# One plan replaced by another: new order, engines and buffer slots for the same instructions of an attention and SwiGLU kernel

## The chip, the core and the metric

The kernel runs on one NeuronCore of a Trainium2 chip. The metric is the device time of one execution in microseconds (us). The core has five engines, each of which works through a queue of its own in order: PE (TensorE, matrix products into PSUM), DVE (VectorE), ACT (ScalarE), POOL (GpSimd) and SP (SyncE, which here only issues DMAs). Engines wait for each other through semaphores. PSUM has eight banks of 128 x 512 float32.

## The reference

Four sequences of 768 positions and eight heads of 64 go through causal attention; heads 0, 2 and 6 see all earlier keys, the others only the first four keys and a window of 64. Its output, 3072 tokens of 512 values, goes through a SwiGLU block of width 1536.

```python
scores = scale * np.matmul(q, k.transpose(0, 1, 3, 2))
...
stream_keep = causal & (is_sink | in_win)
mask = np.where(retr[0, :, 0, 0, None, None], full_mask, stream_mask)
scores = np.where(mask[None, :, :, :], scores, -1000000000.0)
scores = scores - np.max(scores, axis=-1, keepdims=True)
a = np.exp(scores)
a = a / (np.sum(a, axis=-1, keepdims=True) + 1e-09)
return np.matmul(a, v).astype(np.float32)
...
g = x @ w_gate
silu = g * (1.0 / (1.0 + np.exp(-g)))
val = x @ w_val
return (silu * val @ w_out).astype(np.float32)
```

## The kernel before

The work is written as 1071 tasks. `P.add` (in class `Plan`) makes a task with a name, the engines that may do it, what it depends on and the ring of buffers it takes; no task runs at that point. At the end `P.order()` reads three strings: `ORDER` (two characters for each number of a task, in the sequence of emission; numbers from 3700 on are extra warming matmuls), `WAYS` (one digit for each task: which of its engines) and `SLOTS` (one digit for each buffer taken). The loop in the last lines of the kernel emits the tasks in that order. Every engine's queue is therefore the subsequence of `ORDER` that falls to it, and the three strings alone set what waits behind what. Semaphore waits follow from the tiles that tasks share.

Tokens come in 24 tiles of 128 (tile t), two to a pair n (twelve pairs), four to a group g (six groups). A tile's or pair's batch and place follow from `QP`; for instance tiles 8 to 11 are the last four tiles of batch 1 and make group 2, and tiles 12 to 17 belong to batch 2. The tasks' names, as the text uses them:

- `load q5`, `load k5`, `load x5` (x is v), `load g0`, `load v0`, `load o0` (the three weights): DMAs of 512 KB each, issued by SP into a ring of eleven raw buffers (L349 to L362).
- `cq5`, `ck5`, `cx5.0.0`, `wc g0`: casts of raw float32 to float16 (L206 on ACT, L208 on POOL or DVE, L212 as a reduction on DVE).
- `trq`, `trk` and `evq`, `evk`: for pairs 0 to 4, turning of q and k by PE (L473) and evacuation by ACT or DVE. For pairs 5 to 11, `dq5.0`, `dk5.0` are transposing DMAs instead (L463), issued by SP.
- `sc8.0`: scores of a tile, units of up to eight blocks (PE, L567); `ex8.0`: exponentials (ACT, L579); `mask8.0`: product with a 0/1 mask (DVE or POOL, L587); `sk1.2`, `sv1.2`: copies of the sink keys and values into a later tile's place; `val8.1`, `val8.0`: products with v (PE, L597); `nm8`: division by the row sum (DVE, L604 and L605), into a ring of three xb buffers.
- `xtr0` and `xe0`: for tiles 0 to 7, turning of the result by PE (L621) and evacuation. For tiles 8 to 23, `xdma8` is a transposing DMA from SP (L615) into xt.
- `gate2.11`, `vals2.11`: the two products of the SwiGLU block for group 2, column block 11 (PE, L759, four matmuls); `tanh` (ACT, L765), `stt1`, `stt2` (DVE, L769 and L775) make h from them. All gates of a group need the xt of all its four tiles.
- `out1.p1` to `out1.p7`: the output product of a group in seven products by Strassen's scheme (PE, L845, twelve matmuls of 128 x 256 each). `hs1.1` to `hs1.4`, in two parts each (L826, DVE or POOL), are the sums of h that it needs, `ws` (L412) those of w_out; `oe1.r1`, `oe1.c11` and so on gather the products into out_sb (L866 and L859 on DVE, or L206 on ACT); `st1.h0`, `st1.h1` store the halves of a group's result (L883, from SP's or ACT's DMA queue), `st5.*` the pieces of the last group (L874).

PSUM's banks are shared out by `SLOTS`: scores and values take two banks ("big"), a gate, a product or a turning one. Who takes a bank waits until its last user is done with it.

```python
    for number in P.order():
        if number < P.FILL:
            running.append(P.tasks[number])
            P.tasks[number].run()
        else:
            warm((number - P.FILL) % 16, (number - P.FILL) // 16)
```

Of the kernel before, what the change touches and what calls it, by code (L numbers as in the profile page):

```python
# [13 lines left out]


ORDER = (
    "0602070300090A0804010D1U1V1cy11W1X0C1d1f0B2021y01g0g281e1i22231h2B1j290m1r2A0h1Y2C1p1Z1b0F2D1q1a"
    "2L2X0n1s1k1l2N1m2W2M2f051t0G2g1u2O1w2E1v242c2F252h1n1y262d1z272e2i2G2H1o2j0E0z2l2I2P2Q0y2m8o2R2t"
    "2J0k8e118p2K2U8q8f102x2o2V302y8g0i138r8h8s0q318j8i8m2n8k8y323C0H932k8t8l148z3I2p9098943J2S1x9D3D"
    "95918n8u8w929E9G0o388v3K9F3L0j992Z8x963M9H2Y339A0l3R97343U3N1C9B2b2q9C2r0I3S2z9h2u2s3V9c0J2a169i"  # L20
    "3O3W9d9j353P3b369e9N1D373X0r3E3f3l3F393n3m9k0p3Q3g9f3T9O9l3h3Y3Z0s3o9I3a173i9g0K2v1F3j3A190u9L9J"
    "0v3u3d9r2w3c0x3G3k9S0w9K3v9P9Q3H9T9M0M9m9s1G9U3e409t9n431A9R413p9u3B440L9o453q9v429X3r0P4C49464D"
    "3s9Y9V4A9Z189p3t479W4H9a9q2T3x4N4Q4K4B4RBE4V9b4O0tAu1HAzAv48BF0OBH9y3y9zAV4LAw0NB21QB0BG4ZAx4M1R"
    "0R1EAQAy1TB1ApAW4g5D1B4YAY1512AkBI5KAXB4Aq1K4eArB7B51SAZAl0Q9w5CAm0W3zB30SAn3w1M4f4bB9Ao1OAR4h4E"
    "AS4FA44P4I4G5IB69xAa1N5fA54i4lB84j5mAsA01IBAAdAt0Y4mA20V4S4T1J5H5LALA1AbA3AT5G4U5JA74cA8BB5lAcAM"
    "4dBCAU4a1P4JA95gAfBD1LAA5oAg4vAe4kAh5n4q56ANAC57AB0X4r4W5E5F0T514y4o52ADAE4p4nA64sAF4t4zAHAG4w4u"
    "AK545TAI5W5553AOAJ505X4xAiAP5c4X5U58Aj59BL5sBJ5A5tBN5B6wBM5M5p5vBP5NBR0U5YBO0eBKBQ0bBX5q5V6v5r5Z"
    "BV6ICb5hBW6PBU5k5aBZ5bCc6H5OBSBsCd6NCMBt6J5uBuBi745wBYBvBjBaBT6OCNBbBw60CO72CeBcBk71CCCfBlCDBd0a"
    "7PCH0ZBm6QCE666369CI67CJCF7364CK68CG6E5P5QCWCL6A5i5dC75j65815R5x5yCZ5zCX5S61C86UCY6R0fCP6SC96y5e"
    "CaC27OCQ6B62C36e6T6CBn6VC47W6DCABo6F6zBpBx6GCB707F6Z6W0cC56aBhBy7UBq7GC6BzCR6K0dBr6n756X6xCiBe6Y"  # L30
    "6o6M6b6c76CU6fCSD57R77CTD86dDtCVBf7H7879DuC0D6DeBgCk6gC1D7DA7X7A80DjDvDm89CjDkD9DfDl7CDhDnDB857D"
    "DUDgDiDPDV7L6LDWDwDCDQ7b6h83DX6i7ECg7cDYDxDR6k6p7Y6lCm87DS6jCh7I7J7V6qDD7K7M7ZDy7BDE6mDT6rDzDZ86"
    "Cl6sDaE17j6t7dCo7Q6uE0CnDK7NE2DoCpDL88Db7aCsDMDp7sCtDr7tDq7e7m7p7fDN7q7g7nDO7h7rDcEhDdCq7iCuEi7k"
    "Ds7xDFEj82CvCr8I8D8ADGDIDH8B8NCw8J7l7oEwCxDJCyEx7S7T8EEXCz8FEy8G8TEYD0EkE5EZD47u7v8HEz7wE67yD1El"
    "8U8CFLF0D2E3FMFNE88KE48LFB8M8O8V8Q8Y8P8W8RFG847zESE7FH8XFOFCEAEf8ZFPFDFEETF9FFD38SEcEU8aEaEdEe8b"
    "F6Eg8cEuF7FI8dEmE9EBELEEECEbErF1EsEtEFEvF2EVEGEDEpEWEHF8FAEnF4EoFJEqF3EJEIFKFpEKFTGTENGHGUFqGiFr"
    "FsGVF5GbFtEOFVEMGEEPG4GWG5GFG6GYEQFSG7GGGZFUG2GIGaGJGcGOGKG8GMGLGPERGXFzGjGQGRGkGNFQFxFXFRFWG0FY"
    "GSG1FcFaFuFbG9FvFwFiFyG3FeFZFdGdFfFlGeGpGAFjGrGlGBFmGCGfFnGgGDGmFgGhGnFhFkGvGqFoGsGtH1GxGuGzGyGo"
    "GwH3H0HCH2H5H4HAHDH7H8H6HEH9HBHFHG"
)  # L40
WAYS = (
    "000000000000000000000000000000000000000000000000000000000000222222202021222202210011111100110001"
    "212201000100000000000000120002212221011000000000000000001100222210000011000000000001101000000000"
    "001000020202010001000000000000010010010010000000002001020000000000010000012000000100000000000002"
    "000000100000000000200000000000000001020000000010000000000000200000200000000100100000210001001000"
    "000200000020000001001000000001000000100000000001222000000100000000010000102010210000001001000002"
    "200010010000012020212200000010010000000120000001000000000000000000000000000000000000000000000000"
    "000000000000000000000000000000000000000000000000000100000000000000000000000000000000000000000000"
    "000000000000000000000000000000000000000110000000000010000000000000000000000000000000000000000000"
    "000000000000000000001111010011000000000001100000000000000000000000000000000000000000000000000000"  # L50
    "000000000111101000000000000000110000000000000000000000000000000000000000000000000000000000000001"
    "100000110000000000010000000000000000000000000000000000000000000000000000000000000000010000001000"
    "000000000001101"
)
# [1001 lines left out]
```

## Time and profile before

| | us |
|---|---|
| median of 3 runs | 242.46 (241.78 to 242.67) |
| the profiled execution | 242.79 |
| its span, first to last instruction | 241.0 |
| PE busy | 232.1 |
| DVE, ACT, POOL busy | 185.0, 146.0, 127.6 |
| granted TensorE clock, mean | 0.997 |

Times in the trace count from the start of the span. A row of the order of time gives start, length, engine, line, operation, out<-in, form and count, and in brackets how long the engine was idle before it and what ended that. Consecutive like instructions are merged into one row. Issues of DMAs stand under SPq or ACTq: their length is the time in which the queue is held by the issue, not that of the transfer. A row of the waits reads: who waited for whom, us in total, times, longest.

### The profile page before, as it was taken

The numbers are of one execution on the slowest core, as the hardware profiler recorded it, in microseconds if no ns is written. First come the engines' busy times: TensorE is split into PE (matmuls) and PEld (weight loads), VectorE is DVE, ScalarE is ACT, GpSimd is POOL, SyncE is SP. The second block draws the span as 40 slices with busy tenths as digits, with TensorE's granted clock in tenths as the row PEclk, the third lists the DMA queues.
The fourth block names the chain that finished last, engine by engine and source line by source line (L and its number), as shares of the span: only waits on it lengthen the run. The fifth ranks groups of instructions, "written<-read, shape, count | busy, mean of one in ns | idle before, by whom it ended". The sixth has DMA issues, their size and how long they took to land.

```text
span 241.0 us, 5649 instructions
## 1 busy us (share of the span) xinstructions
PE 232.1 (96%) x2211; PEld 146.3 (61%) x2211; DVE 185.0 (77%) x344; ACT 146.0 (61%) x223; POOL 127.6 (53%) x144
## 2 busy tenths in 40 slices
PE   7999999999999998799999999999999999999993
PEld 2677865654566867455564466666746665467783
DVE  2679998989899985498946987568646897875984
ACT  3599999879888878659774684655761111421100
POOL 7395878563957402926969519598960020214220
PEclk9999999999999999999999999999999999999998
DMA  6999999999999979989887414202031000220224
GB/s 184 354 340 366 335 334 366 356 334 305 205 257 167 191 182 252 269 145 213 172 162 223 94 22 89 44 5 77 35 104 51 0 0 0 90 88 0 90 101 162
DMA packets 67179, 40.74 MB, mean 169 GB/s; under 512 B 25168, under 2 KB 61008, under 8 KB 67152
## 3 DMA queue, kind: packets, MB, share of 16 engines
q1 hardware_dynamic: 64832, 36.58, 60.9%
q10 hardware_dynamic: 2320, 3.80, 4.3%
q8 instruction: 17, 0.28, 0.5%
q14 instruction: 10, 0.08, 0.1%
HBM read 28.31 MB, written 6.29 MB: 144 GB/s over the span
## 4 chain that ended last, share of the span: by engine, by line
PE 85%; DVE 5%; DMA 3%; SPq 2%; ACT 1%; issue 1%; POOL 0%; DVEq 0%; POOLq 0%; ACTq 0%
PE banks L759 51%; PE banks L845 17%; PE banks L567 7%; PE banks L597 5%; DMA xt<-xb 3%; PE banks L321 3%; PE banks L473 2%; SPq L615 2%; ACT e L579 1%; DVE out_sb L866 1%; DVE h_sb L775 1%; DVE sil L769 1%; PE banks L621 1%; DVE xb L605 1%; DVE h_sb L826 0%
## 5 line engine op out<-in xcount | busy, mean ns | idle before, releaser
L765 ACT ACTIVATE sig<-banks 128x512 f32<-128x512 f32 (+1 forms) x76 | 42.4, 575 | 53.5 <-PE banks L759 45.9
L759 PE MATMUL banks<-xt,wg_sb 128*128 128x512 f16 (+1 forms) x304 | 71.0, 368 | 1.5 <-DMA xt<-xb 1.5
L759 PE MATMUL banks<-xt,wv_sb 128*128 128x512 f16 (+1 forms) x304 | 71.5, 368 | 0.0
L579 ACT ACTIVATE e<-banks 128x1024 f16<-128x1024 f32 (+2 forms) x68 | 60.0, 912 | 13.4 <-PE banks L567 8.9
L769 DVE SCALAR_TENSOR_TENSOR sil<-sig,banks 128x512 f32<-128x512 f32 (+1 forms) x76 | 48.8, 654 | 15.1 <-ACT sig L765 14.6
L775 DVE SCALAR_TENSOR_TENSOR h_sb<-sil,banks 128x512 f16<-128x512 f32 (+1 forms) x76 | 48.9, 655 | 11.0 <-PE banks L759 9.6
L587 POOL TENSOR_TENSOR e<-e,m 128x640 f16<-128x640 f16 (+1 forms) x22 | 38.0, 1729 | 26.7 <-ACT e L579 24.4
L845 PEld LDWEIGHTS <-h_sb 128*128 128x128 f16 x432 | 41.6, 98 | 9.4 <-DVE h_sb L826 0.2
L759 PEld LDWEIGHTS <-wg_sb 128*128 128x128 f16 x304 | 28.7, 98 | 28.5 <-DMA xt<-xb 1.8
L759 PEld LDWEIGHTS <-wv_sb 128*128 128x128 f16 x304 | 27.9, 98 | 26.8
L826 POOL TENSOR_TENSOR h_sb<-h_sb 128x768 f16<-128x768 f16 x14 | 22.9, 1640 | 31.2 <-DVE hs_sb L826 12.6
L866 DVE TENSOR_TENSOR out_sb<-banks,out_sb 128x512 f32<-128x512 f32 x41 | 27.8, 687 | 7.5 <-PE banks L845 5.8
L845 PE MATMUL banks<-wo_sb,h_sb 128*128 128x256 f16 x216 | 26.4, 273 | 0.0
L845 PE MATMUL banks<-wt_sb,h_sb 128*128 128x256 f16 x216 | 26.3, 273 | 0.0
L567 PE MATMUL banks<-qT,kT 64*128 64x128 f16 x472 | 20.3, 218 | 1.2 <-ACT qT L206 0.6
L567 PEld LDWEIGHTS <-kT 64*128 64x128 f16 x472 | 14.5, 94 | 11.0 <-issue 10.4
L597 PEld LDWEIGHTS <-e 128*128 128x128 f16 x472 | 17.5, 97 | 5.8 <-issue 1.3
L597 PE MATMUL banks<-vt,e 128*128 128x65 f16 x472 | 18.9, 193 | 0.9 <-ACT e L579 0.9
L206 ACT CAST hq<-raw 128x1024 f16<-128x1024 f32 (+1 forms) x17 | 15.9, 945 | 5.2 <-DMA raw<-in_q_dram 4.4
L826 POOL TENSOR_TENSOR hs_sb<-h_sb 128x768 f16<-128x768 f16 x5 | 8.2, 1639 | 20.0 <-DVE h_sb L775 20.0
L605 DVE TENSOR_TENSOR xb<-banks,rc 128x512 f16<-128x512 f32 x24 | 16.6, 691 | 1.8 <-DMA xt<-xb 1.0
L208 POOL CAST vt<-raw 64x512 f16<-64x512 f32 x22 | 13.4, 608 | 2.4 <-DMA raw<-in_v_dram 1.1
(58 smaller groups left out, 185.3 us busy)
## 6 DMA issues: line engine op xcount, KB each, us to landing
raw<-in_v_dram SPq DMA_DIRECT2D x12, 512.0 KB, 6.0
raw<-in_q_dram SPq DMA_DIRECT2D x8, 512.0 KB, 5.2
raw<-in_k_dram SPq DMA_DIRECT2D x8, 512.0 KB, 6.3
raw<-in_moe_w_gate_dram SPq DMA_DIRECT2D x6, 512.0 KB, 8.3
raw<-in_moe_w_val_dram SPq DMA_DIRECT2D x6, 512.0 KB, 8.5
raw<-in_moe_w_out_dram SPq DMA_DIRECT2D x6, 512.0 KB, 8.5
out_dram<-out_sb ACTq DMA_DIRECT2D x6, 512.0 KB, 2.8
raw<-in_q_dram SPq DMA_DIRECT2D x8, 256.0 KB, 6.4
```

The source lines that it names most:

```text
L567: nc.tensor.matmul(sc[:, c:c + n, :], weights, moving, start=first, stop=last)
L579: nc.scalar.activation(out=to, in_=src, func=AF.Exp, scale=scale)
L587: ENG[task().way].tensor_tensor(out=ev, in0=ev, in1=mm, op=ALU.mult)
L597: nc.tensor.matmul(avs[t][:, odd, n * 66:n * 66 + 65], ee, vv, start=(m == 0), stop=(m == len(bl) - 1))
L605: nc.vector.tensor_tensor(out=xb.rearrange("p n o d -> p o n d"), in0=av[:, :, :, 0:64], in1=rc.to_broadcast([128, 2, 4, 64]), op=ALU.mult)
L759: nc.tensor.matmul(ps, wsb[:, kk, j * 128:(j + 1) * 128], xt[:, kk, c[0]:c[1]], start=(kk == 0), stop=(kk == 3))
L765: nc.scalar.activation(out=sg[g, j, c], in_=gs[g, j, c], func=AF.Tanh, scale=0.5)
L769: nc.vector.scalar_tensor_tensor(out=sl[g, j, c], in0=sg.pop((g, j, c)), scalar=1.0, op0=ALU.add, in1=gs.pop((g, j, c)), op1=ALU.mult)
L775: nc.vector.scalar_tensor_tensor(out=hs[g, j][:, c[0]:c[1]], in0=sl.pop((g, j, c)), scalar=0.5, op0=ALU.mult, in1=vs.pop((g, j, c)), op1=A ...
L826: ENG[T_hs[g, x][part].way].tensor_tensor(out=to, in0=a, in1=b, op=op)
L845: nc.tensor.matmul(room[:, n], left[:, j, 128 * x:128 * x + 128], right[:, j], start=(j == 0), stop=(j == NK - 1))
L866: nc.vector.tensor_tensor(out=cell(*to), in0=rooms[g, p], in1=cell(*other), op=ALU.add)
```

## The change

The code stays the same; the three strings are replaced. The first lines of each:

```diff
 ORDER = (
-    "0602070300090A0804010D1U1V1cy11W1X0C1d1f0B2021y01g0g281e1i22231h2B1j290m1r2A0h1Y2C1p1Z1b0F2D1q1a"
...
+    "06000307090A01081U1V0Dy1041W1X0C1c1f1dyG1g0B20211e02280g1i2223052B1j1h0m291p2C0h1Z2A1r1q1a0F2D1Y"
...
 WAYS = (
-    "000000000000000000000000000000000000000000000000000000000000222222202021202222210011111100110001"
...
+    "000000000000000000000000000000000000000000000000000000000000222002202022212202000101001111110120"
...
 SLOTS = (
-    "0014231656750819280736130194319171066202517344332644A5701024020204162213013002411034020501760162"
...
+    "001423105074308961105267896710561344126251638477220387201014020606142212113004411034060501760224"
...
```

Read out, that is: the same 1071 tasks and the same nine extra matmuls; 94 tasks change their engine (ACT has 212 pieces of work after 221, stores included, DVE 310 after 304, POOL 113 after 112, SP 106 after 104, PE 330 as before); 431 of 634 buffers are others; the order differs on every engine. Of the changes of engine these are spoken of below: `hs0.1.0`, `hs0.3.0`, `hs0.4.0`, `hs5.1.0` and `hs5.4.0` from DVE to POOL, nine sums of groups 2 to 5 from POOL to DVE (`hs2.3.0`, `hs2.3.1`, `hs2.2.1`, `hs3.3.0`, `hs3.3.1`, `hs3.2.1`, `hs4.1.1`, `hs4.3.0`, `hs5.3.0`); `oe1.r1` from ACT to DVE; `st0.h1` from SP's DMA queue to ACT's; `sk0.1` from POOL to ACT; `evk1.1` from ACT to DVE; `cx4.0.0` from ACT to POOL; of the last stores, `st5.c21`, `st5.c22` and `st5.c12.1` to SP, `st5.c12.0` to ACT.

SP's queue from load q7 to xdma11, before:

```
load q7, dk5.0, dk6.0, dq5.0, load x6, load x8, load k7, dq5.1, dk5.1, dq6.0, dq7.1,
load k9, load k8, dk6.1, dq6.1, dq7.0, xdma8, dk7.1, dk7.0, load q9, load x7,
st0.h1, st0.h0, xdma10, xdma9, xdma11
```

and after (dq5.0 stands two places ahead of load q7, with load o0 between; load q6 stood ahead of load q7 before):

```
load q7, dq5.1, dk5.0, load k7, load q6, dk5.1, load x6, dk6.0, dq7.0, load k8, load q8,
dk7.1, load k9, xdma8, load x8, dk6.1, dq6.1, dq6.0, load x9, dk7.0, load x10,
xdma9, xdma10, xdma11, then st0.h0, load q9, load x7
```

PE's queue around group 2's first gates, before:

```
out0.p3, sc11.2, sc13.0, sc13.1, vals1.0, vals1.4, val11, sc14.1, out1.p1, sc12.0, sc14.0, sc14.2,
out1.p2, out1.p7, val13.1, out1.p6, gate2.11, val13.0, out1.p4, gate2.2, gate2.8
```

and after:

```
out0.p3, vals1.0, sc11.2, sc13.1, sc13.0, vals1.4, val11, out1.p1, sc12.0, sc14.1, sc14.2, out1.p2,
out1.p4, sc14.0, out1.p7, out1.p6, gate2.2, vals2.2, gate2.8, out1.p5, gate2.11, val13.1
```

In the head, the first fifteen loads keep their order. PE makes sc1.0 ahead of sc1.1 (before: sc1.1 first) and sc2.0 ahead of val1 (before: behind); the first five extra matmuls stand ahead of trq0 instead of behind it. On POOL sk1.1 comes between ck2 and cq2. At the end PE does out5 in the order p1, p4, p2, p6, p7, p5, p3 (before: p1, p2, p7, p6, p4, p5, p3).

More of the change, by code (lines that the diff above doesn't have):

```diff
@@ L16 @@
 ORDER = (
-    "0602070300090A0804010D1U1V1cy11W1X0C1d1f0B2021y01g0g281e1i22231h2B1j290m1r2A0h1Y2C1p1Z1b0F2D1q1a"
[L18 to L36, printed above, removed]
@@ L37 @@
-    "FsGVF5GbFtEOFVEMGEEPG4GWG5GFG6GYEQFSG7GGGZFUG2GIGaGJGcGOGKG8GMGLGPERGXFzGjGQGRGkGNFQFxFXFRFWG0FY"
-    "GSG1FcFaFuFbG9FvFwFiFyG3FeFZFdGdFfFlGeGpGAFjGrGlGBFmGCGfFnGgGDGmFgGhGnFhFkGvGqFoGsGtH1GxGuGzGyGo"
-    "GwH3H0HCH2H5H4HAHDH7H8H6HEH9HBHFHG"
+    "06000307090A01081U1V0Dy1041W1X0C1c1f1dyG1g0B20211e02280g1i2223052B1j1h0m291p2C0h1Z2A1r1q1a0F2D1Y"
+    "2X1s2L0n1b1k2M1l2N1m2f1w2S2E2O0G2W2g1t2h2F1u252c1v1n242d271y262e2i1z2G2j2H1o0E2l0z2I2P2Q2m0y8o2R"
+    "2J2t0k8e8p10118q2x302K8f2U318r8g0i132V8h2y8j0H8i322o8y8k2n3C938s8t2k8m8z148l9D908u3I8n0q948v1x8w"
@@ new lines @@
+    "953D913J982p929E9G380o999F3L3K0J2Y8x969H3M2Z9A333U97343R0l3N1C9B2b2q9C2r0j3V2z9h2u2a3S9c2s160I9i"
+    "359d3O9j3W363T3X3b9I3P370r3F3n3E9e3l3f1D3o399N0M3g2v3Q9k0p2w3h3Y179f9l0K9J3Z9g1F3m9Q9K9O3a3i9r19"
+    "3j0L3d9s3A3k9S3B3G9P9L3v3u9R9m3e9T3c1G9U430t409M0v3H9n9u0x9t442T0u9o3p453q0P1A9v419X3r424Z0w4946"
+    "9Y4C4A9V9Z3y4D3s0N4B9W9p474H9a9q4Y3t4K4N4Q9z4e4L48BE9b3x4MAu4OAnBFAz1HBG9y1BAkAv0sB0BH4P0RAwAxB1"
+    "4fAlBI1518AVAyB21QAW1E4gAXB41SB34RApAm0S3wB7Aq0O5D124h4EAY1RB54FA4B6A04I0QAZ4b5KAo9w5f1TArB8AQ5l"
@@ new lines @@
+    "4V4G1OATAR3z9x0V4i4lAS0U4jB9A2AU4mAaA1Ad4nAb1KBA4S1MAs5gA31NAL1I5C5oAc1J4TBBBC4W4U0Y4kA84JAtAM5G"
+    "A5AA0W5FAN1L5L4vBDAf1PA95J56AgAB4qA6AC57Ae5I4rAh4dA74o4yAD514a0ZAE4p5n524sAF4t0c4zAH534XAG4w504u"
+    "AOAKAI544x5W5T6K55Ai4cAP5U5H58Aj595cBJ5X5ABL5B5M5s5vBMBN5tBRBOAJ0X5NBQBZBP0T5V0e6H5p5mBX5qBK5r7Q"
+    "BVBsBW5EBSBvBtBUBY6I6OCMBu6vBbBa0aBTBwCN71Cb5kCO5Y5ZBdCc6NCe5wCdBi5hBc6P6w5aBjCC5b0b5dBlCfCD7460"
+    "5uBkCH6LCE72CFCIBm5O5j6669CJ6367CGCK645i5P5QC75R815xCLC85y5S68CW61C9C25z73CX6ECZ65CYC36Q6ACPCa7P"
@@ new lines @@
+    "6R6UCQ0d6z6B6S5e6C6xCA6D6V6J62Bn6eCB6TC4BxBo6GBp6Z7F6X6aBqBy0f7S7GBzC07O6YC5C16y7UBr6F6n7C756oC6"
+    "7VCR6W6bCSD57X76CT6c7WD8D6777DCUBhBeCVD7CjDeBfD978DjDf7H7TDgDtDk6d8079DhDu6f6g6M83Dw7LDlCiDm88Di"
+    "DvDP7EDxDUDQ7ABgDADVDR7B707b6hDnDBCgDW7c89DC6iClDXCh6k6p7YDY6qCkDDCn7ICm7J6lDSDE7KDo7Z6m7NCs7jDT"
+    "87DyCt6jDZDzDpE0Co7RDa6rCp6sCqDc6tE17dDq6u7s7eE27tDr7a867M7fCuDsDbCr7m7pCv7nDKDd7g7xDLEh82DM7hEi"
+    "DN7i7qDFDO7rEj8A8I8D8JCy8B7o7kCwDG8C7uDH7vDICx7y7wEz7l8E8ND0EXDJD48G8TCzE58HE384EY8UEZ8FEw8KExD1"
@@ L40 @@
+    "E6Ey8LD2FL8O8MFOFMF08PE48Y8WFN8Q8V8X7zEcFPEaE8FBEbE7FEFCEAEdEkFD8ZFFEB8REl85EfEED3EeESE9FGEgEFEC"
+    "F68SEGFJF7FHF88aErFIEuFKEsET8bF18cEHED8dEUEtEmF2EvELEnEIF9EVEJGEEKF3EpENEOEWFAGTEoG4GYG5GUG6F4EM"
+    "GFG7EqERFsF5FSGdGGGHGVFTGMG8FpFVEPGOFUGIGWGPGZGQGJGaFiGKGXEQFqFYFrFtFQFuFXFRGLGeFbGbFZFvFxGNGiFw"
+    "FWG2FyFaGcG9FzFeG0G1FcG3GAGfGRFdGjFlGkFfGlFjGSGgGmGpGCGhGBFgGDFmGnFhFnFkH3GqFoGrGvGsGtGuGzGyGoH1"
+    "H0GxGwH5H2HCH4HAH6HDH8H7HBHEH9HGHF"
 )
 WAYS = (
-    "000000000000000000000000000000000000000000000000000000000000222222202021222202210011111100110001"
@@ L43 @@
[L43 to L52, printed above, removed]
@@ L53 @@
-    "000000000001101"
+    "000000000000000000000000000000000000000000000000000000000000222002202022212202000101001111110120"
+    "122100101100000000000000220002212221011001000000000000001100222210000011000000000001101000000000"
+    "001000020202010001000001000000001000000010000000002020210000000000010000002000100100000120020020"
+    "000000100000000000200010000000000002200200000010000000001000210002200000000100100000220001001000"
+    "001101021000000001000000000010000000000000000022222000000000000010010002002011200000001001000000"
@@ new lines @@
+    "200010010000012022221000000010010000000110000000000000000000000000000000000000000000000000000000"
+    "000000000000000000000000000000000000000000101000001100000000000010000000000000000000000000000000"
+    "000000000000000000000000000000100000000110000000000010000000000000000000000000000000000000000000"
+    "000000000000000000001100000011000000000001000000000000000000000000000000000000000000000000000000"
+    "000000000110000000000000000000110000000000000000000000000000000000000000000000000000000000000000"
@@ L54 @@
+    "000000110000000000010000000000000000000000000000000000000000000000000000000000000001000000011000"
+    "000000000000010"
 )
 SLOTS = (
-    "0014231656750819280736130194319171066202517344332644A5701024020204162213013002411034020501760162"
-    "640031200305410001604412220022054023444270112442300420022145012100434405620062034100306201145640"
-    "041032124622005626103610064626106064032162414162610561104522030114064414134422500032200212345414"
-    "114211500050013400631272017410570216113500060267122601760114127065323261037024212670027012402600"
@@ L60 @@
-    "164024600311023110711545464637007410300005110502420135015410451232100510471141107650100450216117"
-    "612201001105300631041020201321142100666624501057023111220062101502141173025012771036017101112140"
-    "6131114013402040145127712270231115700510230011600471064140"
+    "001423105074308961105267896710561344126251638477220387201014020606142212113004411034060501760224"
+    "616061236065010005244410263006054144604161076240041410052243400140614523412064214222322202163402"
+    "101244163404500616213234064010206120024422206342404542326543624212462202021256022432243646022204"
@@ L63 @@
+    "010500100012020011241034023311121203007100760173106202730202111303601071212001112220017110201710"
+    "260023110631063112601610254571104212211133100101331205023210201102116010341201444401312231111005"
+    "110211002020510061267010101121030104514154751061006011400160003402600247121611110070001002167232"
+    "5160044103611450150114202331025124610700161003701235412321"
 )
```

## Prediction

> **What bounds the kernel now.** I read the page's head and the windows by stage first, then all waits of PE, then PE's and SP's instructions in order of time where PE stood still.
>
> ```profile
> span 241.0 us, 5649 instructions
> ...
> 0.00:20.00 20.00, 17.88 (x213) 11.24 (x214) 11.04 (x27) 13.57 (x19) 13.84 (x38) 1.00 0.97 299
> ...
> 60.00:84.00 24.00, 24.00 (x247) 16.07 (x246) 22.34 (x42) 20.37 (x31) 16.38 (x15) 1.00 1.15 209
> 84.00:99.00 15.00, 11.92 (x152) 8.66 (x150) 8.97 (x17) 11.43 (x16) 4.05 (x3) 1.00 1.00 213
> 99.00:200.00 101.00, 100.97 (x914) 60.00 (x913) 74.76 (x133) 57.49 (x89) 60.11 (x51) 1.00 0.43 96
> ```
>
> A window row gives its length, the busy time of PE, PEld, DVE, ACT and POOL, and the granted clock. PE is the bound: it does not rest from 60 to 84 and hardly from 99 to 200, at clock 1.00. The change keeps every matmul, so only PE's idle time can go: 2.1 us before 20, 3.1 in 84 to 99, and what follows the last matmul.
>
> ```profile
> PE banks L759 <- DMA xt<-xb: 1.5, 1, 1.5
> PE banks L321 <- POOL ident L234: 1.4, 1, 1.4
> PE banks L597 <- ACT e L579: 0.9, 1, 0.9
> PE banks L567 <- ACT qT L206: 0.6, 1, 0.6
> PE banks L567 <- DVE xb L605: 0.6, 1, 0.6
> ```
>
> These are all of PE's waits in the list. The 1.4 stands ahead of the first matmul, which the change leaves; the 0.6 behind ACT is in the head. The other three are these, followed by two rows from the end that give the pace of a product:
>
> ```profile
> 84.50 0.62 PE L567 MATMUL banks<-qT,kT 64*128 64x128 f16 x14
> 85.70 0.40 PE L567 MATMUL banks<-qT,kT 64*128 64x128 f16 x8 [0.59 <-DVE xb L605]
> ...
> 92.44 1.47 PE L845 MATMUL banks<-wt_sb,h_sb 128*128 128x256 f16 x12
> 94.86 0.40 PE L597 MATMUL banks<-vt,e 128*128 128x65 f16 x8 [0.94 <-ACT e L579]
> 95.10 1.47 PE L845 MATMUL banks<-wt_sb,h_sb 128*128 128x256 f16 x12
> 98.11 1.02 PE L759 MATMUL banks<-xt,wg_sb 128*128 128x512 f16 x4 [1.54 <-DMA xt<-xb]
> ...
> 227.91 2.78 PE L845 MATMUL banks<-wo_sb,h_sb 128*128 128x256 f16 x24
> ...
> 235.85 1.47 PE L845 MATMUL banks<-wo_sb,h_sb 128*128 128x256 f16 x12
> ```
>
> A wait costs more than its idle time, since the pipeline drains. Six products of twelve matmuls lie between 227.91 and 235.85: 1.32 each from start to start. The product at 92.44 is followed after 2.42, so **1.1** is lost; that at 95.10 after 3.01, so **1.7** is lost; the fourteen score matmuls at 84.50 fill about 0.5 of their 1.20, **0.7** lost. Together **3.5 us**. All three come out of SP's one queue:
>
> ```profile
> 56.44 3.06 SPq L354 DMA_DIRECT2D raw<-in_q_dram  x1
> 59.63 3.88 SPq L463 DMA_TRANSPOSE kT<-hq  x2
> ...
> 67.87 2.45 SPq L463 DMA_TRANSPOSE qT<-hq  x1
> 70.37 1.27 SPq L463 DMA_TRANSPOSE kT<-hq  x1
> ...
> 74.89 1.23 SPq L354 DMA_DIRECT2D raw<-in_k_dram  x2
> 76.17 2.39 SPq L463 DMA_TRANSPOSE kT<-hq  x1
> 78.61 2.58 SPq L463 DMA_TRANSPOSE qT<-hq  x2
> 81.29 1.21 SPq L615 DMA_TRANSPOSE xt<-xb  x1
> ...
> 87.08 1.70 SPq L883 DMA_DIRECT2D out_dram<-out_sb  x2
> 88.83 6.02 SPq L615 DMA_TRANSPOSE xt<-xb  x3
> ...
> 93.64 4.34 DMA xt<-xb
> ...
> ACT out_sb L206 <- DMA out_dram<-out_sb: 1.1, 1, 1.1
> ```
>
> SP issues almost back to back here. xdma8 goes out at 81.29; nm10 (L605) waits for its buffer, and sc13.1 for nm10's bank: the wait at 85.70. The two stores go out at 87.08; oe1.r1 on ACT waits 1.1 for one to land, ex14.0 stands behind it on ACT, and val13.1 needs ex14.0's bank: the wait at 94.86. xdma11, last of the three at 88.83, goes out at 93.64 and lands 4.34 later (the chain's row): the wait at 98.11.
>
> **The change, part by part.**
>
> *SP's queue up to xdma11.* From 59.63 to 94.85 SP made 25 issues, sixteen transposes and nine plain ones, in 35.2 us. Plain ones took 0.6 to 0.85 (74.89, 87.08), gaps 0.05; with 6.3 and 1.2 for these, a transpose took (35.2 - 7.5) / 16 = 1.7 on average. The first behind two or more plain issues took 2.4 (67.87, 76.17), one directly behind another 1.25 (70.37, 78.61, 81.29). The new queue has fourteen transposes and nine loads from load q7 to xdma11: dq7.1, loads q9 and x7 and both stores no longer stand there, dq5.0 has gone ahead of load q7; loads q6, q8, x9 and x10 are new there. At the average that is 14 x 1.7 + 9 x 0.6 + 23 x 0.05 = 30.4. But loads are strewn in singly, so that there are eight runs of transposes; if each run's head takes 2.42 and the other six 1.25, it is 26.9 + 6.6 = 33.5. Load q7 is issued at 56.44 + 3.06 = 59.5, so xdma11 is out between 89.9 and 93.0. It lands later by 2.8 to 4.34: **92.7 to 97.3**. I take 95, as the backlog ahead is two loads instead of two loads and two stores. PE wants it at 98.11 - 3.5 + 1.1 = 95.7, since product p4 (1.32) now stands ahead of group 2's first gate and val13.1 (0.2) behind it. Value: no wait; bounds 0 and 1.6.
>
> xdma8 is the seventh of the fourteen, behind six loads. At most that is 5 x 2.42 + 2 x 1.25 + 6 x 0.6 + 12 x 0.05 = 18.8 behind 59.5: out by 78.3, landed by 82.6 with 4.34. PE asks for what follows nm10 at 85.0. The 0.7 goes; next latest is nm10 itself, now behind two gathers and a mask on DVE.
>
> *st0.h1 goes to ACT's queue, oe1.r1 from ACT to DVE, val13 behind group 2's first gates.*
>
> ```profile
> out_dram<-out_sb ACTq DMA_DIRECT2D x6, 512.0 KB, 2.8
> ```
>
> From ACT's queue a store lands 2.8 after its issue, and it is issued right behind sv1.4, not behind SP's loads. oe1.r1 lands on DVE, which is busy 8.97 of 15 in that window. The 1.1 goes. If the store came late all the same, oe1.r1 would hold up DVE's casts behind it, with cover on PE: four pieces of group 2 and product p5 now stand between p6 and val13.1.
>
> *Three hs0 sums go from DVE to POOL.*
>
> ```profile
> L826 POOL TENSOR_TENSOR h_sb<-h_sb 128x768 f16<-128x768 f16 x14 | 22.9, 1640 | 31.2 <-DVE hs_sb L826 12.6 <-PE banks L845 7.4 <-DVE h_sb L826 6.9
> L826 DVE TENSOR_TENSOR h_sb<-h_sb 128x768 f16<-128x768 f16 x10 | 5.5, 552 | 1.6 <-PE banks L845 1.5
> ...
> POOL e L587 <- ACT e L579: 13.9, 1, 13.9
> ```
>
> In 60 to 84 DVE was busy 22.34 of 24. It is relieved by 3 x 0.55 = 1.7; POOL takes 3 x 1.64 = 4.9 and has 13.9 of idle time right behind. What is hidden by this is not free everywhere: cx4.0.0 now stands on POOL behind hs0.1.0, and val8, which needs it, comes 3.7 earlier on PE. sc13.1, sc10.3 and val11 also follow their last producer closely. I count 0.5 given back at such places; the bounds are 0 and one whole sum, 1.6.
>
> *POOL's pieces may meet DVE's.*
>
> ```profile
> 23.95 1.09 DVE L587 TENSOR_TENSOR e<-e,m 128x640 f16<-128x640 f16 x2
> ...
> 24.57 1.36 POOL L208 CAST wv_sb<-raw 128x1024 f16<-128x1024 f32 x1 [1.82 <-DMA raw<-in_moe_w_val_dram]
> ...
> L208 POOL CAST wg_sb<-raw 128x1024 f16<-128x1024 f32 x4 | 4.1, 1037 | 0.5 <-DMA raw<-in_moe_w_gate_dram 0.4
> ```
>
> A POOL cast that met a DVE mask took 1.36 where its like take 1.04: 0.3 dearer. Cost taken: 0 beyond the 0.5; the other end is a rival below. [...]
>
> *The head.*
>
> ```profile
> 12.88 3.77 ACT L579 ACTIVATE e<-banks 128x1024 f16<-128x1024 f32 x4
> ...
> 17.74 1.07 ACT L206 COPY qT<-banks 128x512 f16<-128x512 f16 x2
> ...
> 18.37 0.40 PE L567 MATMUL banks<-qT,kT 64*128 64x128 f16 x8 [0.60 <-ACT qT L206]
> ```
>
> ACT's four exponentials (0.94 each) and the evacuation of q2 set when PE goes on at 18.37. PE now makes sc1.0 ahead of sc1.1, in ACT's order, so ACT can begin up to one unit earlier. But sk0.1 joins ACT in this stretch, evk1.1 goes from ACT to the end of DVE's evacuations, so that sc3.0 comes later, and on POOL sk1.1 stands ahead of cq2. The first fifteen loads keep their order. I take 0; bounds: the whole wait of 0.6 with its drain (0.8) won, one unit (0.9) lost.
>
> *99 to the end.* PE idled 0.03 in 101 us, while DVE, ACT and POOL had 26, 44 and 41 free: nothing to win, and cover for what moves. At the end both hs5.4 sums go to POOL and p2 comes third: it ends at 227.91 + 3 x 1.32 = 231.9, two sums of 1.64 at 235.2, p3 wants them at 235.85. Cost 0, with 0.6 of cover; each us beyond it counts in full.
>
> **Sum.** 242.79 (the profiled execution: span 241.0, and 1.8 around it) - 3.5 + 0.5 + 0 = 239.8. The median shown, 242.46, is 0.3 below that execution, so **239.5**; this case's own range is 238.6 to 240.7 (head won, or 1.2 more given back).
>
> **Rivals.**
>
> *Group 2 still waits.* xdma11 at 97.3 or SP a little later: 1 to 2.5 come back, 240.5 to 242, about 241.4. For it: eight runs of transposes. Against: the smaller backlog. Chance 0.14.
>
> *The head slips* by its 0.9: 240.4. Chance 0.06.
>
> *DVE shuts POOL out* at the narrow places (val8, val11, hs5.4): three or four meetings at 0.3 to 0.6, 240.6 to 242. The trace bears out the price, not where the new order meets. Chance 0.10.
>
> *Slower: the mixed queue issues slowly.* Should the fourteen transposes take 2.42 each, loads between or not, they make 33.9 + 6.6 = 40.5; xdma11 is out at 100 and lands at 102.8, 7 late: **246**. It decides from 2.14 each: out at 96.1, landed at 98.9, 3.2 late, and the gain is gone. For it: 2.4 behind loads, and more such places. Against: 1.7 on average, 1.25 without loads. Chance 0.12.
>
> The forecast has 0.58. That nothing changes is no case: every engine's order does.
>
> **How the numbers follow.** About 0.5% (1.2 us) is what a measurement of this kernel can tell from no change: the borders are 241.25 and 243.7. Faster: 0.58, the head's 0.06, and 0.05 each of group 2 and the lock: 0.74. Same: 0.09 and 0.05 of these two, and 0.01 of the slow queue: 0.15. Slower: 0.11 of the slow queue. The range 238.6 to 242.2 leaves out that 0.11 and some 0.05 on the other side.
>
> **What would show it.** Right: PE's list of waits loses its rows on xb, on xt and on e; PE is busy throughout 84 to 99; xdma11 lands by 96; POOL's wait of 13.9 shrinks. Wrong: a new PE wait on POOL e or h_sb (POOL late, or shut out), one on DMA xt (the queue), or a first gate (L759) well behind the 20 us at which the first window ends (the head).

## The result and the profile after

| | before | after |
|---|---|---|
| median, us | 242.56 (241.78 to 242.69) | 239.58 (239.41 to 240.66, 4 runs) |
| ratio, 95% interval | | 0.9896 [0.9872, 0.9921] |
| the profiled execution, its span | 242.79, 241.0 | 240.66, 238.8 |
| PE busy | 232.1 | 232.2 |

Faster by 1.0%, 3.0 us. The profiled execution of after is the slowest of its four; the other three lie between 239.41 and 239.66. All waits of PE in the list, after:

```profile
PE banks L321 <- POOL ident L234: 1.4, 1, 1.4
PE banks L473 <- DVE sil L769: 0.5, 1, 0.5
PE banks L621 <- DVE xb L605: 0.4, 1, 0.4
PE banks L567 <- DVE kT L208: 0.3, 1, 0.3
```

The rows on xt, on e and on xb behind L567 are gone. The 1.4 stands as before; the 0.4 and the 0.3 are in the head. The 0.5 is new. The windows of after, with the same columns as in the forecast:

```profile
20.00:60.00 40.00, 39.49 (x432) 24.76 (x428) 34.34 (x71) 36.67 (x59) 28.67 (x32) 1.00 1.11 334
60.00:84.00 24.00, 24.00 (x235) 15.57 (x234) 19.46 (x38) 20.05 (x31) 17.94 (x17) 1.00 1.04 245
84.00:99.00 15.00, 15.00 (x182) 11.18 (x179) 13.54 (x25) 9.18 (x14) 6.94 (x6) 1.00 1.03 228
```

From 84 to 99 PE works without a rest (15.00, before 11.92), and DVE is busy for 13.54 (before 8.97), POOL for 6.94 (4.05). From 60 to 84 DVE has 19.46 (22.34). The half microsecond that PE lacks from 20 to 60 is the new wait. SP's queue in order of time, after:

```profile
69.85 0.63 SPq L354 DMA_DIRECT2D raw<-in_q_dram  x1
74.10 1.20 SPq L463 DMA_TRANSPOSE kT<-hq  x1
75.40 0.53 SPq L354 DMA_DIRECT2D raw<-in_k_dram  x1
76.02 1.22 SPq L615 DMA_TRANSPOSE xt<-xb  x1
...
85.39 6.05 SPq L615 DMA_TRANSPOSE xt<-xb  x3
91.49 1.99 SPq L883 DMA_DIRECT2D out_dram<-out_sb  x1
```

xdma8 goes out at 76.02, the three of group 2 from 85.39 to 91.44, the first store behind them. SP does not issue back to back here: ahead of 74.10 it stood still for 3.62, until the cast ck7 on ACT had ended, and ahead of xdma11 for 1.08, until nm11 on DVE had. PE at that place:

```profile
92.40 1.47 PE L845 MATMUL banks<-wt_sb,h_sb 128*128 128x256 f16 x12
93.81 0.40 PE L567 MATMUL banks<-qT,kT 64*128 64x128 f16 x8
94.14 2.79 PE L845 MATMUL banks<-wt_sb,h_sb 128*128 128x256 f16 x24
96.77 1.03 PE L759 MATMUL banks<-xt,wg_sb 128*128 128x512 f16 x4
```

Group 2's first gate starts at 96.77 without a wait; xdma11 landed at 94.80, 4.55 after its issue at 90.25.

### The profile page after: what moved, and what is told of

Same layout as the page of the kernel before. It is cut to its first block, busy times and chain, and to the rows that moved or that the text cites. A ratio compares the mean times of both kernels' runs of the same rounds, so it can differ in the third digit from the quotient of the medians.

```text
span 238.8 us, 5641 instructions
## 1 busy us (share of the span) xinstructions
PE 232.2 (97%) x2211; PEld 145.9 (61%) x2211; DVE 187.3 (78%) x348; ACT 141.1 (59%) x217; POOL 126.0 (53%) x146
## 4 chain that ended last, share of the span: by engine, by line
PE 84%; DVE 9%; issue 2%; POOL 2%; ACT 1%; DMA 1%; DVEq 0%; POOLq 0%; ACTq 0%
PE banks L759 50%; PE banks L845 16%; PE banks L567 7%; PE banks L597 6%; PE banks L321 3%; DVE out_sb L866 3%; PE banks L473 2%; DVE h_sb L775 2%; POOL e L587 1%; DMA out_dram<-out_sb 1%; DVE sil L769 1%; DVE kT L208 1%; ACT sig L765 1%; PE banks L621 1%; DVE qT L208 1%
## 5 line engine op out<-in xcount | busy, mean ns | idle before, releaser
L579 ACT ACTIVATE e<-banks 128x1024 f16<-128x1024 f32 (+2 forms) x68 | 59.4, 909 | 15.7 <-PE banks L567 13.6
L826 POOL TENSOR_TENSOR h_sb<-h_sb 128x768 f16<-128x768 f16 x11 | 17.9, 1643 | 58.9 <-DVE h_sb L826 48.6
L587 POOL TENSOR_TENSOR e<-e,m 128x640 f16<-128x640 f16 (+1 forms) x22 | 38.6, 1762 | 15.8 <-ACT e L579 8.8
L759 PEld LDWEIGHTS <-wg_sb 128*128 128x128 f16 x304 | 28.2, 98 | 26.0
L597 PEld LDWEIGHTS <-e 128*128 128x128 f16 x472 | 18.2, 97 | 6.7 <-POOL e L587 0.7
L567 PEld LDWEIGHTS <-kT 64*128 64x128 f16 x472 | 14.5, 94 | 10.3 <-issue 9.1
L567 PE MATMUL banks<-qT,kT 64*128 64x128 f16 x472 | 20.3, 218 | 0.1
L597 PE MATMUL banks<-vt,e 128*128 128x65 f16 x472 | 19.9, 193 | 0.1
L826 POOL TENSOR_TENSOR hs_sb<-h_sb 128x768 f16<-128x768 f16 x6 | 9.9, 1643 | 13.0 <-DVE h_sb L775 12.9
L208 POOL CAST vt<-raw 64x512 f16<-64x512 f32 x24 | 14.5, 607 | 1.8 <-DMA raw<-in_v_dram 0.7
L208 POOL CAST hq<-raw 128x1024 f16<-128x1024 f32 (+1 forms) x13 | 12.2, 939 | 4.5 <-ACT sig L765 1.7
```

The lines of the kernel that those rows point to most:

```text
L208: ENG[task.way].tensor_copy(out=dst, in_=src)
L567: nc.tensor.matmul(sc[:, c:c + n, :], weights, moving, start=first, stop=last)
L579: nc.scalar.activation(out=to, in_=src, func=AF.Exp, scale=scale)
L587: ENG[task().way].tensor_tensor(out=ev, in0=ev, in1=mm, op=ALU.mult)
L597: nc.tensor.matmul(avs[t][:, odd, n * 66:n * 66 + 65], ee, vv, start=(m == 0), stop=(m == len(bl) - 1))
L759: nc.tensor.matmul(ps, wsb[:, kk, j * 128:(j + 1) * 128], xt[:, kk, c[0]:c[1]], start=(kk == 0), stop=(kk == 3))
```

## The experiments

Queues are given as lists of tasks, the part that is moved with + and -. All ratios are against the kernel before on the same chip.

| kernel | median (lowest to highest) | ratio, 95% interval |
|---|---|---|
| after_again | 239.58 (239.50 to 239.67) | 0.9878 [0.9858, 0.9898] |
| mask_first | 240.10 (239.91 to 240.26) | 0.9899 [0.9880, 0.9917] |
| head_fill | 239.51 (239.32 to 239.76) | 0.9878 [0.9852, 0.9905] |
| stores_ahead | 239.72 (239.45 to 240.37) | 0.9888 [0.9865, 0.9911] |
| loads_ahead | 242.99 (241.27 to 244.51) | 1.0013 [0.9984, 1.0042] |
| hs0_dve | 240.89 (240.55 to 241.24) | 0.9932 [0.9911, 0.9954] |
| hs034_dve | 240.65 (240.29 to 241.36) | 0.9932 [0.9901, 0.9963] |
| before_sp | 243.15 (241.93 to 244.88) | 1.0030 [1.0004, 1.0056] |
| before_hs0 | 242.85 (241.87 to 245.01) | 1.0020 [0.9991, 1.0049] |
| before_order | 246.48 (244.97 to 247.96) | 1.0166 [1.0126, 1.0206] |
| before_joint | 246.92 (246.05 to 248.91) | 1.0189 [1.0153, 1.0225] |
| before_acts | 242.53 (241.03 to 244.74) | 0.9993 [0.9960, 1.0027] |

**Is the new wait at 26 us a cost of the plan?** Three engines of after in order of time:

```profile
24.43 1.04 POOL L208 CAST wv_sb<-raw 128x1024 f16<-128x1024 f32 x1 [1.83 <-DMA raw<-in_moe_w_val_dram]
24.45 1.55 DVE L587 TENSOR_TENSOR e<-e,m 128x1024 f16<-128x1024 f16 x1
26.39 0.61 PE L473 MATMUL banks<-ident,hq 128*128 128x128 f16 x8 [0.51 <-DVE sil L769]
```

POOL's cast of a weight began 26 ns before DVE's mask4.0 (24.429 and 24.455 in the trace). The mask took 1.55 instead of 0.69, DVE was late with the piece whose bank trq3 takes, and PE lost 0.67 there. The plan was run again unaltered (after_again), and once with the mask behind xe3 on DVE (mask_first).

> The changed kernel once more, unaltered. Of its four executions one took 240.66 us, the profiled one, and three 239.4 to 239.7. In the profile mask4.0 on DVE (L587, at 24.45) took 1.56 us where its like take 0.69, because a cast on POOL had begun 26 ns before it; PE then waited 0.5 us for a bank. Theory (who starts first shuts the other out, so the two outcomes differ by chance): a profile of an execution near 239.5 shows mask4.0 at 0.7 us and the cast at 1.3 to 1.4, and no PE wait at L473; one near 240.6 shows the first picture again. Rival (the 1.1 us comes from elsewhere, the start-up DMAs say): mask4.0 takes 1.56 us in an execution near 239.5 too.

```diff
 DVE of after (mask_first):
+mask4.0 behind xe3
 stt2 0.0.0, mask5.1, mask4.1, stt2 0.1.0,
-mask4.0,
 stt1 0.0.256
```

> The changed kernel with one move on DVE: mask4.0 directly behind xe3, some 1.7 us earlier, ahead of POOL's cast of v1. Theory: no 1.56 us mask, no PE wait at L473, all executions at 239.2 to 239.7; in the profile PE stands still 0.7 to 1.1 us less between 20 and 37 than in the profile of the changed kernel. Rival (the meeting costs PE nothing): the same median and the same spread up to 240.7 as the changed kernel.

The same three engines in after_again:

```profile
24.17 0.69 DVE L587 TENSOR_TENSOR e<-e,m 128x1024 f16<-128x1024 f16 x1
24.70 1.06 POOL L208 CAST wv_sb<-raw 128x1024 f16<-128x1024 f32 x1 [1.85 <-DMA raw<-in_moe_w_val_dram]
25.43 0.61 PE L473 MATMUL banks<-ident,hq 128*128 128x128 f16 x8
```

DVE came first by 0.53, the mask took 0.69, the cast 1.06 (not the 1.3 to 1.4 expected), and PE did not wait here: a span of 237.7 instead of 238.8. The list of after_again has a wait of 0.5 for POOL instead, but at trk0, in the head. Of the 1.1 between the spans, 0.67 is this wait and 0.29 was lost before group 0's first gate. Of the seven profiles in which the mask stands at this place on DVE (after, after_again, head_fill, stores_ahead, loads_ahead, hs0_dve, hs034_dve), only that of after has it held up; and of the eight executions of the unaltered plan one took 240.66, the others 239.41 to 239.67. So the wait is a matter of chance of single executions and no fixed cost of the plan. mask_first has no such wait in its profile either, and the narrowest spread but one, but its median is 0.5 above after_again, against what was expected. PE lost 0.3 more in its head, 0.2 at gate0.2 (23.75), whose bank comes free by a piece that now stands behind the mask, and 0.2 at sc20.1 (135.4). The middle one is a price of the move; the other two are open.

head_fill moved mfill1 (the fill of a mask) on DVE behind cx0.1.1, out of the evacuations of the head.

```diff
 DVE of after:
 ck1.1,
-mfill1,
 evk0.1, evq1.0,
...
 evk1.1, cx0.0.0, cx0.1.1,
+mfill1,
 nm0
```

> The changed kernel with mfill1 (0.6 us on DVE) moved from ahead of evk0.1 to behind cx0.1.1; the masks that it fills are first used at 23 us. PE lost 0.24 at trk1 or sc1.0, 0.4 at sc3.0 behind evk1.1 and 0.5 at xtr1 in the profiles. If DVE's evacuations set the head: 0.3 to 0.5 us won, 239.1 to 239.3. If ACT's exponentials or DMA set it: 239.5 as before.

PE's loss at sc3.0 fell from 0.40 to 0.19, but 0.3 turned up at sc20.1 (135), and the time stayed.

**Does SP's queue set group 2's first gate in the new plan?** Two doses of the old order were put back.

```diff
 SP of after:
 load x10,
+st0.h1, st0.h0,            (both kernels)
+load q9, load x7,          (loads_ahead alone)
 xdma9, xdma10, xdma11
-st0.h0, load q9, load x7   (as far as moved)
 ACT of after:
 sv1.4,
-st0.h1,
 ex11.2
```

> The changed kernel with the two stores of group 0 put back on SP's queue ahead of xdma9 to xdma11, all else as it is. Queue theory: xdma11 lands 2.5 to 3.2 us later, at 97.3 to 98, PE waits 0.6 to 1.2 for it at group 2's first gate, 240.3 to 240.8 in all. Rival (the gain came from DVE's relief by the hs0 sums, not from the queue): no wait, 239.5 within 0.3.

> The new plan with four DMAs put ahead of xdma9 on SP: st0.h1, st0.h0, load q9 and load x7. This is the dose behind stores_ahead, where the two stores alone made xdma11 land 2.24 us later (95.91) and PE lost 0.38 at group 2's first gate. Theory (SP's queue still sets the first gate of group 2, with about 1.9 us of slack in the new plan): two loads more bring two issues of 0.6 and 512 KB each, about 3 us of landing, so xdma11 lands near 99, PE waits some 3 us on xt, and the time is 242.0 to 243.3. Rival (the slack of the new plan covers it, other work comes due elsewhere): xdma11 lands before 97 and the time stays under 240.7.

The stores alone moved xdma11's landing from 93.67 (after_again) to 95.91, and PE waited for it:

```profile
PE banks L759 <- DMA xt<-xb: 0.2, 1, 0.2
```

0.38 was lost and the time hardly moved, less than expected; 239.72 is within the 0.3 that the rival allowed. The new plan has about 1.9 us to spare here. With the loads as well, first the wait of PE, then the issue, then PE in order of time:

```profile
PE banks L759 <- DMA xt<-xb: 3.0, 1, 3.0
```

```profile
89.44 8.11 SPq L615 DMA_TRANSPOSE xt<-xb  x3
...
98.89 1.02 PE L759 MATMUL banks<-xt,wg_sb 128*128 128x512 f16 x4 [2.95 <-DMA xt<-xb]
```

The three transposes are out at 97.55 instead of 91.44, and all of the gain is gone (1.0013). Part of that is the granted clock (last section): the six executions at 0.997 or more took 241.27 to 242.60, median 242.07, which is 2.5 above after_again. In the new plan the queue's order is necessary for the gain.

**What are the hs0 sums on POOL worth?** The forecast priced them at no gain.

```diff
 DVE of after:
 stt2 0.7.0,
+hs0.1.0,                   (hs0_dve alone)
 stt1 1.11.0,
...
 stt1 1.1.0,
+hs0.3.0,
 hs0.2.0,
...
 hs0.2.1,
+hs0.4.0,
 ws2.1
 POOL of after:
-hs0.1.0 (hs0_dve alone), hs0.3.0, hs0.4.0
```

> The changed kernel with hs0.1.0, hs0.3.0 and hs0.4.0 back on DVE. Queue theory: DVE has 4.5 of 24 us free from 60 to 84 and takes the 1.7 us; 239.3 to 240.1. Rival (the relief of DVE is what made the gain): 1 to 2 us slower, 240.5 to 241.5, with PE waits on DVE between 60 and 99.

> The changed kernel with hs0.3.0 and hs0.4.0 back on DVE, hs0.1.0 left on POOL. All three back cost 1.3 us, and there hs0.1.0 or hs0.1.1 on DVE took 2.1 us instead of 0.55 because POOL's mask9.0 had begun before it. If the lock was the price: no such instruction here, 239.4 to 239.9. If DVE's load was: two thirds of the price stay, 240.2 to 240.6.

hs0_dve is 1.3 above after_again, the rival's side. Its DVE and POOL in order of time:

```profile
53.26 3.80 POOL L587 TENSOR_TENSOR e<-e,m 128x1024 f16<-128x1024 f16 x2 [2.01 <-ACT e L579]
53.70 2.10 DVE L826 TENSOR_TENSOR hs_sb<-h_sb 128x768 f16<-128x768 f16 x1
```

One sum on DVE took 2.10 instead of 0.55 behind a mask of POOL. In hs034_dve, with hs0.1.0 on POOL, none is held up so, and it is still 1.1 above. Its waits:

```profile
PE banks L759 <- DVE sil L769: 0.3, 1, 0.3
...
PE banks L759 <- DVE h_sb L775: 0.3, 1, 0.3
```

PE loses 0.42 at vals1.3 (71.3) and 0.50 at vals1.10 (75.1) in both. DVE works almost without a rest from 67 to 77, and the pieces that free these two banks, stt2 of 1.1 and stt1 of 1.3, stand behind hs0.3.0 and hs0.4.0 in its queue. So it is the two sums' place in DVE's queue that costs, not the meeting with POOL. The busy share does not show it: over 60 to 84 DVE has 19.99 of 24 here and 20.09 in after_again.

**Do the parts gain anything on the old plan?** Five kernels put parts of the change into the old strings.

```diff
 SP of before:
+xdma8,
 dk6.1, dq6.1, dq7.0,
-xdma8,
 dk7.1, dk7.0,
-load q9, load x7,          (not in before_sp)
-st0.h1, st0.h0,
 xdma10, xdma9, xdma11
+st0.h0                     (before_sp, before_order, before_joint)
+load q9, load x7           (not in before_sp)
 ACT of before:
 sv1.4,
+st0.h1,
 ex11.2, ex13.1, sk2.1, ex13.0,
+st0.h0,                    (before_acts alone)
 ex14.1
 PE of before (before_order, before_joint):
 out1.p7,
-val13.1,
 out1.p6,
+out1.p4,
 gate2.11,
+val13.1,
 val13.0,
-out1.p4,
 gate2.2, gate2.8,
+out1.p5,
 gate2.0, vals2.2,
-out1.p5
 DVE to POOL (before_joint; before_hs0 has this alone):
 hs0.1.0, hs0.3.0, hs0.4.0
```

> The kernel before, with three moves in its queue of DMAs and nothing else: st0.h1 from SP's queue to ACT's, st0.h0 from ahead of xdma10 to behind xdma11, xdma8 ahead of dk6.1. Queue theory: PE's waits on xb (0.6) and on ACT e (0.9) go, xdma11 lands at 95 to 96.5 and 0 to 1.5 of its 1.7 us stay: 239.5 to 240.8. Rival (the relief of DVE by the hs0 sums is needed): DVE still delivers nm10 and nm11 late, under 1 us gained, 241.5 or more.

The waits of PE in before_sp:

```profile
PE banks L759 <- DMA xt<-xb: 1.9, 1, 1.9
PE banks L321 <- POOL ident L234: 1.4, 1, 1.4
PE banks L845 <- DVE out_sb L866: 1.2, 1, 1.2
...
PE banks L567 <- DMA kT<-hq: 0.4, 1, 0.4
```

The waits on xb and on e are gone; that on xt stays, as the two loads still stand ahead of xdma11 (out at 93.39, landed at 96.98). st0.h0 now lands at 98.74, and a new wait on out_sb comes with it. Not faster: what was expected of the queue alone did not come.

> The kernel before, with hs0.1.0, hs0.3.0 and hs0.4.0 on POOL and nothing else. Queue theory: the three waits in 84 to 99 hang on SP and stay; 241.8 to 242.6. Rival (DVE's relief made the gain): 240 to 241.

No gain either (1.002). PE still lost 1.29 at val13.1 and 0.61 at group 2's first gate (nothing at sc13.1, which it reached later), and new losses stand inside out0.p6 (75.1, 1.0) and at vals2.2 (103.9, 1.3). Three pieces of DVE were held up by one of POOL, the longest a sum of 1.99, and out0.p6 waited for it. The sum on DVE, the one on POOL and PE:

```profile
72.47 1.99 DVE L826 TENSOR_TENSOR h_sb<-h_sb 128x768 f16<-128x768 f16 x1
72.36 1.70 POOL L826 TENSOR_TENSOR h_sb<-h_sb 128x768 f16<-128x768 f16 x1 [1.49 <-DVE h_sb L826]
75.11 1.16 PE L845 MATMUL banks<-wt_sb,h_sb 128*128 128x256 f16 x9 [0.87 <-DVE h_sb L826]
```

> The old plan with the queue part and PE's order around group 2 together: st0.h1 to ACT's queue behind sv1.4, xdma8 ahead of dk6.1, and st0.h0, load q9 and load x7 behind xdma11 on SP; on PE out1.p4 ahead of gate2.11, out1.p5 behind gate2.8, val13.1 behind gate2.11. The hs0 sums stay on DVE. Theory (the three waits are what the gain is made of, and the queue alone failed only since two loads still stood ahead of xdma11): xdma11 lands by 95, the waits on xb, e and xt go, 2 to 3 us are won: 239.6 to 240.8. Rival (the gain needs DVE's relief, or the work that came late in the earlier trial comes late again, as oe1.c11 did): 241.6 to 243.

> As before_order, and hs0.1.0, hs0.3.0 and hs0.4.0 on POOL as in the new plan. Theory (the sums on POOL pay about 1.1 us once the queue no longer hides it, as hs0_dve showed from the other side): 0.5 to 1.3 below before_order, 239.0 to 240.3. Rival (on the old plan these sums meet DVE's and lock it out, as in before_hs0): equal to before_order or up to 1 above it, 240.0 to 243.

Both missed by far. before_order, DVE and PE in order of time:

```profile
95.67 0.69 DVE L866 TENSOR_TENSOR out_sb<-banks,out_sb 128x512 f32<-128x512 f32 x1 [2.73 <-DMA out_dram<-out_sb]
96.41 1.47 PE L845 MATMUL banks<-wt_sb,h_sb 128*128 128x256 f16 x12 [1.18 <-DVE out_sb L866]
...
104.23 1.47 PE L845 MATMUL banks<-wt_sb,hs_sb 128*128 128x256 f16 x12 [2.02 <-DVE out_sb L866]
```

DVE (oe1.r6) stands still for st0.h0, and p4 waits for the bank that oe1.r6 frees. p5 waits for another, that of oe1.r67; this comes late behind a tanh of ACT, as in the last kernel below. In the old `SLOTS` p1, p6 and p4 take the same bank, each after the gather (oe1.r1, oe1.r6) of the one before; in the new strings p4 takes that of sc14.1, p6 that of sc14.0. So p4 ahead of the gate is of use only with the new banks. As both kernels tested this fault more than the theory, the last one left PE's order alone and gave both stores to ACT.

> The old plan with SP's queue cleared and both stores early: st0.h1 on ACT's queue behind sv1.4, st0.h0 on ACT's queue behind ex13.0, load q9 and load x7 behind xdma11 on SP, xdma8 ahead of dk6.1. Nothing else moves; PE's order and the hs0 sums are the old ones. In before_sp and before_order, st0.h0 came late behind xdma11 and DVE stood still for it; here it does not. Theory (the three waits came out of SP's queue and nothing else): the waits of PE on xb, ACT e and DMA xt shrink to under 1 in all, xdma11 lands by 95.5, and the time is 239.6 to 240.6. Rival (the queue alone is not enough, since DVE and the old banks hold the same stretch): 241.6 or more, with new PE waits on out_sb, sil or h_sb.

PE of before_acts in order of time:

```profile
90.00 0.39 PE L567 MATMUL banks<-qT,kT 64*128 64x128 f16 x7 [1.49 <-DMA kT<-hq]
...
95.03 0.40 PE L597 MATMUL banks<-vt,e 128*128 128x65 f16 x8
95.27 1.47 PE L845 MATMUL banks<-wt_sb,h_sb 128*128 128x256 f16 x12
96.58 1.03 PE L759 MATMUL banks<-xt,wg_sb 128*128 128x512 f16 x4
...
101.63 1.02 PE L759 MATMUL banks<-xt,wg_sb 128*128 128x512 f16 x4 [0.75 <-DVE sil L769]
103.20 1.02 PE L759 MATMUL banks<-xt,wv_sb 128*128 128x512 f16 x4 [0.55 <-DVE sil L769]
```

val13.1 (95.03) and the first gate of group 2 (96.58) go without a wait, and sc13.1 too: **the three old waits are gone**. In their place PE loses 0.54 at sc13.0, which waits for a transposed q, 1.72 around sc14.1 (90.00), which waits for the transposed k of pair 7, and 1.62 at two pieces of group 2 (101.63, 103.20). Together 3.9 after 3.6 (start to start, counted as in the forecast). The k that sc14.1 needs, dk7.0, went out at 85.83, since xdma8 stands ahead of it, and landed at 89.95; before, at 84.47 and 87.21. The two late pieces wait for DVE, DVE for a tanh of ACT, and ACT stood for load q9:

```profile
97.10 1.99 ACT L206 CAST hq<-raw 128x1024 f16<-128x1024 f32 x2 [2.25 <-DMA raw<-in_q_dram]
99.00 1.24 ACT L206 CAST vt<-raw 64x512 f16<-64x512 f32 x2
100.26 0.60 ACT L765 ACTIVATE sig<-banks 128x512 f32<-128x512 f32 x1
```

The old plan has the casts cq9, ck8 and those of x7 ahead of group 2's first tanh on ACT. The new one has the tanh first, as ACT of after_again shows:

```profile
96.72 0.60 ACT L765 ACTIVATE sig<-banks 128x512 f32<-128x512 f32 x1 [2.56 <-PE banks L759]
97.34 1.99 ACT L206 CAST hq<-raw 128x1024 f16<-128x1024 f32 x2
```

There the load can come late at no cost to group 2. The median of before_acts is that of before, but its executions differ in the granted clock (last section): seven at 0.997 or more took 241.03 to 242.88, median 241.40, and five at 0.991 to 0.993 took 243.34 to 244.74. The profile is that of the slowest of the seven. So even with the clock undisturbed the cleared queue wins some 1.3 us on the old plan (242.71 on that chip), less than half of the gain. No run put the old plan's order of ACT or its banks into the new plan, or the new ones into the old: that these make up the rest is read from the traces and not shown by a run.

## Why the prediction was right, and where not

The time came out as forecast (239.5, measured 239.58), and by the chain that carried most of the sum. The signs named for it came as well: the three rows are gone, PE is busy throughout 84 to 99, xdma11 landed by 96, and POOL's longest wait for e fell from 13.9 to 2.4.

- **SP's queue up to xdma11**: right in its times, but two terms were off and in part made up for each other. xdma11 was forecast out between 89.9 and 93.0 and landed between 92.7 and 97.3, with 95 taken; it was out at 91.44 and landed at 94.80. xdma8, at most 78.3 and 82.6, came at 77.24 and 80.22. The term of 1.7 for a transpose was too large: the fourteen took 20.7 in all, 1.48 each (1.62 in after_again). The term for the gaps, 23 x 0.05 = 1.2, was far too small: they came to 7.3 (4.7 in after_again), since SP waited for casts and for nm11. The sum counted an old queue that never waits; that the new one came out within its bounds is in part luck. xdma11 itself was held by nm11 on DVE in the end, not by the DMAs ahead of it. The 4.34 to its landing, besides, counts from the start of an issue and was added to its end. The slower rival, which decides from 2.14 for a transpose, was well off.
- **The gain of 3.5**: right in size and place. Counted from start to start, PE lost 0.81, 1.10 and 1.71 at sc13.1, val13.1 and gate2.11 before, 3.6 in all, and nothing at their places after. The step "All three come out of SP's one queue" was half of the truth. The waits do come from there: before_acts empties them, loads_ahead brings the one on xt back and the gain is lost. But what was taken off the front of that queue was due elsewhere: on the old plan it cost as much again in the profiled execution, and in the median of the undisturbed ones more than half of it. The new plan can pay for it, as the traces have it, because ACT's order and the banks were planned with it; the forecast looked at PE's order around these places and gave no term to the other two.
- **The hs0 sums**: mis-sized. They were priced as cover, at 0 gain and 0.5 given back. On DVE in the new plan they cost 1.1 to 1.3 (hs034_dve, hs0_dve). The forecast gave their removal no worth, because PE did not wait in that window before. In the new plan's order two of the pieces behind them free a bank just as PE asks for it, so that each sum of 0.55 comes out as a wait (0.42 and 0.50 lost in hs034_dve).
- **The 0.5 given back**: nearly the right size, at other places. At val8, sc10.3, sc13.1 and val11 nothing was lost. The span fell from 241.0 to 238.8 in after's profile and to 237.7 in after_again, by 2.2 and 3.3 of the 3.6: 1.4 given back elsewhere in the one, 0.3 in the other. The difference is mostly the meeting at 24.43.
- **The head**: 0 was right. Group 0's first gate starts at 19.88 before, at 19.93 after and at 19.64 in after_again, behind as many matmuls of the same forms.
- **The rival on DVE and POOL**: its price of 0.3 was measured in one order, DVE first (1.36 for 1.04, before). POOL first, DVE lost 0.86 (1.55 for 0.69, after) and 1.55 (2.10 for 0.55, hs0_dve). In these three the one that began later was held up. hs034_dve sets a limit to this reading: there the cast began 9 ns ahead of the mask by the trace, and yet it was the cast that stood still (1.59). So the order of the recorded starts alone does not tell who is held up. The 0.6 at the upper end of the rival's price no run had shown; in the traces of before and after a piece of POOL lost at most 0.40 behind a mask on DVE (a copy at 31.93 in after, 0.85 for 0.45), in hs034_dve the cast lost 0.55.
- **99 to the end**: as forecast, nearly. Up to 200 PE idled 0.06 of 101 us (0.03 before), and from its last matmul to the end of the span it was 3.81 (3.67 before).

## What to carry to other kernels

A wait that ends on a transfer names the queue, not the cure: before a DMA is moved back, look up what it feeds and where that consumer stands on its own engine, or the wait turns up there (before_acts lost 3.9 where before had lost 3.6). Parts of a plan that are worth little or nothing on the old one (0.9993 for the queue, 1.002 for the sums) can carry all or a third of the gain in the new one (loads_ahead, hs034_dve), so a plan isn't judged by its parts alone. An engine's busy share doesn't tell whether one more piece is free: 0.55 us on DVE cost nearly as much on PE (0.42 and 0.50) with DVE busy for 20 of 24 us, because the piece behind it was just due.
